# A weight loaded in halves, slot logits spread over two pairs, and zero products in the tail of an attention and mixture-of-experts kernel

## The chip, the cores and the metric

The kernel runs on one core of a Trainium2 chip. A core has TensorE (PE: matrix products, with weight loads shown as PEld), VectorE (DVE), ScalarE (ACT), GpSimd (POOL) and SyncE (SP), which run their own instruction streams and wait for each other by semaphores, and 16 DMA engines that serve all queues. The metric is the device time of one execution in microseconds (us); runs of one kernel are told by their median. The profile is of one execution; its span reaches from the first to the last instruction.

## The reference

Two layers follow each other. The first is causal attention over 4 batches, 8 heads, 768 positions and 64 columns, where some heads see all earlier positions and the others only the first 4 and the last 64. The second is a soft mixture of experts over all 3072 tokens of 512 columns, with 8 experts of 4 slots each:

```python
x = attention(q, k, v).transpose(0, 2, 1, 3).reshape(B * S, H * D)
logits = x @ phi                                   # 3072 x 32
slot_input = softmax(logits, axis=0).T @ x         # 32 slots x 512
for e in range(8):
    h = maximum(slot_input[e] @ w1[e], 0)          # 4 x 1024
    slot_out[e] = h @ w2[e]                        # 4 x 512
out = softmax(logits, axis=1) @ slot_out           # 3072 x 512
```

The slot softmax runs over all tokens, so no expert can start before attention has ended. The inputs are float32: q, k and v have 18.9 MB, w1 and w2 together 33.6 MB. The output has 6.3 MB.

## The kernel before

**Attention** runs over 16 pairs of heads (`n`, four to a batch). A pair's scores are cut into six groups (`g`): `qk` makes the scores of one group and their exponentials on ACT (lines 116 to 135), `mask` zeroes what a head does not see (DVE), and `pvmm` multiplies by v with an appended column of ones (line 159). q, k and v come with rows in partitions and are turned on PE: `transpose` (line 85) into a PSUM tile of the pool `trp`, which has two buffers and serves seven kinds of tile in rotation, and `evac` copies it to SBUF. While pair `n` is computed, q, k and v of pair `n + 1` are turned, in groups 2, 3 and 4; the transposes follow the group's scores and precede its value products. `norm` divides by the column of sums into `xb`, the attention output; `x_transpose` and `evac_x` make its transpose `xT`, one pair behind.

**Slot work inside the loop.** Batch `b` is done when pair `4b + 3` is. In the following pairs, with `bt = (n - 4) % 4`, its logits are made: `slot_logits(b, c)` (lines 188 to 201) multiplies phi by half of `xT` on PE, takes the exponential on ACT and copies it on POOL into `expT`. Both halves run in the pair with `bt == 1`, after groups 0 and 3. `xT` has one buffer. `slots_to_tokens(b)` turns the exponentials (six small transposes) in group 1 of the pair with `bt == 2`, and `dispatch(b)` uses them with `xb` in group 1 of the pair with `bt == 3`. The last batch has a way of its own behind the loop.

**Order.** The order of each engine's instructions is written out by hand. Loads other than the first q and phi are issued from POOL's queue, which casts them to bf16, in program order: k and v of pair 0, the identity (a memset and a select), q, k and v of pair 1, those of pairs 2 and 3 in one transfer each, then one weight at the head of most pairs (`w_order`, line 311) and the loads of two later pairs at the head of odd pairs. The buffers of q, k and v lie in what are w2[5] to w2[7] later, so these three weights are issued last, after the transposes of pair 15. w2[6] and w2[7] come in halves of 256 columns: both left halves, then both right ones. A weight w1 lands with 8,192 B to a partition.

**The tail.** `layer1` makes the hidden rows of all experts from w1, `h_transpose` turns them, and `layer2(e, c0, cl)` adds eight products of expert e into one PSUM tile `sp` (line 575). When the left half of w2[7] has been used, `slot_cols(0)` scales the left half of the slot outputs on ACT (line 599), `row_sums` makes the token sums of a batch by six products with one column (line 271), and `piece` multiplies `expT` by `slot_out` (line 614), scales on ACT and DVE by turns (lines 617 and 619) and issues the output from SP (line 620). The left halves of batches 0 and 1 are written first, then the right halves, then batches 2 and 3 in whole rows. `warm(count, cols)` issues products of a tile of zeros into a tile that nobody reads.

Of the kernel before, what the change touches and what calls it, by code (L numbers as in the profile page):

```python
# [35 lines left out]
class Attn:  # L36
    def __init__(self, nc, tc, ctx, q, k, v, env):
        self.nc, self.tc = nc, tc
        self.src = {"q": q, "k": k, "v": v}
        self.__dict__.update(env)  # L40
        ent = ctx.enter_context
        self.qkT = ent(tc.tile_pool(name="qkT", bufs=2))
        self.vTp = ent(tc.tile_pool(name="vTp", bufs=1))
        self.ptp = ent(tc.tile_pool(name="ptp", bufs=4))
        self.small = ent(tc.tile_pool(name="small", bufs=2))
        self.xp = ent(tc.tile_pool(name="xp", bufs=2))
        self.xTp = ent(tc.tile_pool(name="xTp", bufs=1))
        self.scp = ent(tc.tile_pool(name="scp", bufs=2, space=PSUM))
        self.trp = ent(tc.tile_pool(name="trp", bufs=2, space=PSUM))
        self.pvp = ent(tc.tile_pool(name="pvp", bufs=1, space=PSUM))  # L50
        self.rawt, self.tp, self.T, self.pT, self.pv = {}, {}, {}, {}, {}
        self.xb, self.xT, self.esl, self.elg, self.lg = {}, {}, {}, {}, {}
# [223 lines left out]
def kernel(  # L276
# [23 lines left out]
    w1s = [singles.tile([P, 4, F], BF16, name=f"w1_{e}") for e in range(NE)]  # L300
    w2s = [singles.tile([P, 8, DM], BF16, name=f"w2_{e}") for e in range(NE)]

    def w_load(i, c0=0, cl=DM):
        if i < NE:
            nc.gpsimd.dma_start(w1s[i], moe_w1[i].rearrange("(di do) f -> di do f", do=4))
        else:
            nc.gpsimd.dma_start(w2s[i - NE][:, :, c0:c0 + cl],  # L307
                                moe_w2[i - NE].rearrange("(fi fo) d -> fi fo d", fo=8)[:, :, c0:c0 + cl])


    w_order = [(i,) for i in range(2 * NE - 2)] + [
        (i, c, DM // 2) for c in (0, DM // 2) for i in (2 * NE - 2, 2 * NE - 1)]

    ident = singles.tile([P, P], BF16, name="ident")
# [15 lines left out]
    with ExitStack() as actx:  # L330
        asing = actx.enter_context(tc.tile_pool(name="asing", bufs=1))
        slot_acc = asing.tile([P, DM], F32, name="slot_acc")
        slot_bf = asing.tile([P, DM], BF16, name="slot_bf")
# [17 lines left out]
        at = Attn(nc, tc, actx, q, k, v, env)  # L351
# [14 lines left out]
        nc.gpsimd.memset(ident, 1.0)  # L366
        nc.gpsimd.affine_select(ident, ident, pattern=[[-1, P]], compare_op=ALU.is_equal,
                                fill=0.0, base=0, channel_multiplier=1)
        at.load(1)
        at.load(2, pairs=2)  # L370

# [50 lines left out]
        for n in range(NP):  # L422
            if n % 2 and n + 3 < NP:
                at.load(n + 3, pairs=2)
            for _ in range(0 if n % 4 == 3 or n > 13 else len(w_order) - 5 if n == 13 else 1):
                w_load(*w_order.pop(0))
            if n == 1:

                nc.gpsimd.memset(sum4, 1.0)
                for g in range(4):  # L430
                    nc.gpsimd.affine_select(sum4[32 * g:32 * (g + 1)], sum4[32 * g:32 * (g + 1)],
                                            pattern=[[-1, ES]], compare_op=ALU.is_equal,
                                            fill=0.0, base=0, channel_multiplier=1)
                phf = at.small.tile([P, 4, ES], F32, tag="eb", name="phf", bufs=1)
                nc.sync.dma_start(phf, moe_phi.rearrange("(do di) s -> di do s", di=P))
            for g in range(NG):

                if n or g != 1:
                    at.qk(n, g)
                if n == 0 and g == 0:  # L440
                    at.qk(n, 1)
                last = n == NP - 1

                b, bt = (n - 4) // 4, (n - 4) % 4 if n >= 4 else 0
                if g == 0:
                    if n == 0:
                        at.transpose(0, "v")
                        at.evac(0, "v")
                    else:
                        at.pvmm(n - 1, 4)  # L450
                        at.v_blocks(n)
                        at.evac_blocks(n)
                    at.mask(n, 0)
                elif g == 1:
                    if n:
                        at.pvmm(n - 1, 5)
                    else:
                        at.v_blocks(n)
                        at.evac_blocks(n)
                    if bt == 2:  # L460
                        at.slots_to_tokens(b)
                    elif bt == 3:
                        at.dispatch(b, slot_bf if last else None)
                    if n:
                        at.norm(n - 1, 1)
                elif g == 2:
                    if not last:
                        at.transpose(n + 1, "q")
                    at.pvmm(n, 0)
                    at.mask(n, 1)  # L470
                    if not last:
                        at.evac(n + 1, "q")
                elif g == 3:
                    if not last:
                        at.transpose(n + 1, "k")
                    at.pvmm(n, 1)
                    at.mask(n, 2)
                    if not last:
                        at.evac(n + 1, "k")
                elif g == 4:  # L480
                    if not last:
                        at.transpose(n + 1, "v")
                    at.pvmm(n, 2)
                    if not last:
                        at.evac(n + 1, "v")
                elif g == 5:
                    if n:
                        at.x_transpose(n - 1)
                    at.pvmm(n, 3)
                    if n:  # L490
                        at.evac_x(n - 1)
                    at.norm(n, 0)
                if n == NP - 2 and g == NG - 1:
                    for w in w_order:
                        w_load(*w)
                if n == 0 and g < 2:
                    at.warm(2)
                if bt == 1 and g in (0, 3):
                    at.slot_logits(b, g // 3)
                if (n, g) in MASK_AT:  # L500
                    head_mask(MASK_AT[n, g])
                if n == 2 and g == 0:
                    nc.vector.tensor_copy(phi4.rearrange("p d (g s) -> p d g s", g=4),
                                          phf.rearrange("p d (g s) -> p d g s", g=1).to_broadcast([P, 4, 4, ES]))
                if n == 3 and 2 <= g:
                    gg = g - 2
                    for e4 in range(2):
                        s0 = SPE * (4 * e4 + gg)
                        nc.vector.reduce_sum(emask[32 * gg:32 * (gg + 1), e4:e4 + 1],
                                             sum4[32 * gg:32 * (gg + 1), s0:s0 + SPE], axis=AX.X)  # L510
        n, b = NP - 1, B - 1
# [59 lines left out]
        def layer2(e, c0=0, cl=DM):  # L571
            e4, g = e // 4, e % 4
            for fo in range(8):
                r = fo % 4
                nc.tensor.matmul(sp[32 * r:32 * (r + 1), c0:c0 + cl], hT[e4][:, fo, 32 * g:32 * (g + 1)],
                                 w2s[e][:, fo, c0:c0 + cl], start=(e == 0 and fo < 4),
                                 stop=(e == NE - 1 and fo >= 4), skip_group_check=True)
# [19 lines left out]
        def slot_cols(c):  # L597

            nc.scalar.activation(slot_out[:, 256 * c:256 * (c + 1)], sp[:, 256 * c:256 * (c + 1)], ACT.Copy, scale=rcol)  # L599
# [20 lines left out]
            nc.sync.dma_start(ov[:, r:r + m, c0:c0 + cl], ot[:, o:o + m, c0:c0 + cl])  # L620

        HALF = DM // 2
        for e in (NE - 2, NE - 1):
            layer2(e, 0, HALF)
        slot_cols(0)
        for b in range(2):
            at.row_sums(b)
        for b, r, m in ((0, 0, 1), (0, 1, 2), (0, 3, 3), (1, 0, 3), (1, 3, 3)):
            piece(b, r, m, 0, HALF)
        for b in range(2, B):  # L630
            at.row_sums(b)
        for e in (NE - 2, NE - 1):
            layer2(e, HALF, HALF)
        slot_cols(1)
        for b, r, m in ((0, 0, 1), (0, 1, 2), (0, 3, 3), (1, 0, 3), (1, 3, 3)):
            piece(b, r, m, HALF, HALF)
        for b in range(2, B):
# [37 lines left out]
```

## Time and profile before

| | |
|---|---|
| Median of six runs | 152.33 us (152.13 to 152.92) |
| The profiled execution | 152.92 us, span 151.2 us |
| PE / ACT / DVE / POOL busy | 131.0 / 114.3 / 115.3 / 42.0 us |
| Queue 0 (POOL's loads) | 26.02 MB written, 94.6% of 16 engines' span |
| Queue 1 (SP's loads and outputs) | 6.76 MB, 12.6% |
| HBM read, written | 52.50 MB, 6.29 MB |
| Score exponentials on ACT (lines 129, 133) | 44.3 + 51.8 us |

The page shows the span in 40 slices of 3.78 us. A busy share above 1 for DMA means that packets overlap. The GB/s of a load are counted on the side that is written, in bf16, so that the float32 read is twice as much. The chain of waits follows the last instruction back to what released it at each step. In a timeline a row has start, duration, engine, line, operation, tiles written and read, and in brackets the idle time of the engine before it with what ended it.

### The profile page before, as it was taken

To read this page: it belongs to the slowest core of one execution; us is meant where nothing else is said; L and a number is where in the kernel's file an instruction comes from. 1 tells how busy PE (TensorE), PEld (TensorE's weight loads), DVE (VectorE), ACT (ScalarE), POOL (GpSimd) and SP (SyncE) were. 2 spreads that over 40 slices of the span, in tenths; PEclk is the share of its full clock that TensorE was granted. 3 is DMA by queue.
4 is the path that set the end of the run, shared out by engine and by line. 5 is a ranking of instruction groups with operands and counts; after the bars stand their busy time and mean duration, and the time that the engine had idled before them with its cause. 6 is when DMAs were issued, how large, how long until landed. Compare 5 with 4: busy or idle time off the path is not lost.

```text
span 151.2 us, 5388 instructions
## 1 busy us (share of the span) xinstructions
PE 131.0 (87%) x2312; PEld 83.0 (55%) x2313; DVE 115.3 (76%) x280; ACT 114.3 (76%) x187; POOL 42.0 (28%) x63
## 2 busy tenths in 40 slices
PE   6999898997999999999999999899788992989500
PEld 2457566664657756665775766577364451654100
DVE  6889999899897998988789898788955430548700
ACT  3379899998989999998998999899961530649600
POOL 7917404202455410335554010456400000000000
PEclk9999999999999999999999999999999999556975
DMA  4999999999999999999999999999999999998994
GB/s 112 137 189 206 234 191 213 223 215 203 205 225 198 209 228 219 194 213 224 195 216 220 219 198 208 222 215 212 221 217 215 197 194 197 146 340 296 395 414 187
DMA packets 20327, 33.12 MB, mean 219 GB/s; under 512 B 1616, under 2 KB 17808, under 8 KB 18512
## 3 DMA queue, kind: packets, MB, share of 16 engines
q0 software_dynamic: 15616, 26.02, 94.6%
q1 hardware_dynamic: 4688, 6.76, 12.6%
q8 instruction: 18, 0.29, 0.7%
q14 instruction: 5, 0.04, 0.1%
HBM read 52.50 MB, written 6.29 MB: 389 GB/s over the span
## 4 chain that ended last, share of the span: by engine, by line
DMA 43%; PE 20%; DVE 19%; issue 7%; ACT 3%; POOL 2%; DVEq 0%; POOLq 0%; ACTq 0%
DMA w<-in_k_dram 25%; DMA w<-in_moe_w_dram 16%; PE op L614 4%; DVE xb L172 3%; PE pv L159 3%; DVE pT L143 3%; DVE pT L146 3%; PE sc L124 3%; DVE vb L113 2%; DMA w<-in_q_dram 2%; PE ls L192 2%; PE tpv L85 2%; DVE w L619 2%; DVE xT L186 1%; ACT pT L133 1%
## 5 line engine op out<-in xcount | busy, mean ns | idle before, releaser
L133 ACT ACTIVATE pT<-sc,fb 128x512 bf16<-128x512 f32 (+1 forms) x96 | 51.8, 618 | 3.5 <-PE sc L124 3.0
L129 ACT ACTIVATE pT<-sc 128x1024 bf16<-128x1024 f32 (+1 forms) x48 | 44.3, 953 | 2.7 <-PE sc L124 2.3
L159 PE MATMUL pv<-vb,pT 128*128 128x65 bf16 x672 | 37.0, 194 | 4.2 <-DVE pT L143 2.7
L124 PE MATMUL sc<-qT,kT 64*128 64x256 bf16 (+3 forms) x320 | 34.8, 280 | 0.1
L159 PEld LDWEIGHTS <-pT 128*128 128x128 bf16 x672 | 26.3, 97 | 15.4 <-issue 6.3
L85 PEld LDWEIGHTS <-w 96*64 96x64 bf16 x768 | 19.3, 110 | 11.6 <-issue 8.5
L146 DVE TENSOR_TENSOR pT<-pT,msk 128x1024 bf16<-128x1024 bf16 (+1 forms) x32 | 19.6, 614 | 0.0
L172 DVE TENSOR_TENSOR xb<-pv,rs 128x384 bf16<-128x384 f32 x32 | 17.8, 557 | 1.1
L201 POOL COPY expT<-esl 128x384 bf16<-128x384 bf16 x6 | 11.5, 1910 | 16.5 <-ACT esl L198 16.5
L124 PEld LDWEIGHTS <-kT 64*128 64x128 bf16 x320 | 10.8, 94 | 8.9 <-issue 3.4
L186 DVE COPY xT<-tpx 128x768 bf16<-128x768 bf16 (+1 forms) x17 | 9.1, 535 | 6.8 <-PE tpx L180 6.8
L76 POOL DMA_DIRECT2D w<-in_q_dram x8 | 5.5, 684 | 31.1 <-PE tpq L85 27.7
L143 DVE TENSOR_TENSOR pT<-pT,msk 128x1024 bf16<-128x1024 bf16 x16 | 11.7, 733 | 0.7 <-ACT pT L129 0.7
L619 DVE TENSOR_SCALAR w<-op,rrow 128x256 f32<-128x256 f32 (+1 forms) x18 | 9.5, 570 | 2.9 <-PE op L614 2.7
L101 DVE COPY vT<-tpv 128x768 bf16<-128x768 bf16 x16 | 8.8, 549 | 3.1 <-PE tpv L85 3.0
L614 PE MATMUL op<-slot_out,expT 128*128 128x256 bf16 (+1 forms) x36 | 9.6, 395 | 0.8 <-ACT slot_out L599 0.6
L617 ACT ACTIVATE w<-op,rrow 128x256 f32<-128x256 f32 (+1 forms) x18 | 9.3, 545 | 1.4 <-PE op L614 1.1
L307 POOL DMA_DIRECT2D w<-in_moe_w_dram x10 | 6.7, 675 | 9.5 <-DMA w<-in_moe_w_dram 4.3
L85 PE MATMUL tpk<-ident,w 96*64 96x96 bf16 x256 | 8.5, 209 | 0.7 <-DMA w<-in_k_dram 0.7
L113 DVE COPY vb<-tpb 128x768 bf16<-128x768 bf16 x16 | 8.9, 558 | 0.1
L85 PE MATMUL tpq<-ident,w 96*64 96x96 bf16 x256 | 8.8, 214 | 0.2 <-DVE w L396 0.2
L85 PE MATMUL tpv<-ident,w 96*64 96x96 bf16 x256 | 8.5, 209 | 0.0
(93 smaller groups left out, 148.6 us busy)
## 6 DMA issues: line engine op xcount, KB each, us to landing
w<-in_moe_w_dram POOLq DMA_DIRECT2D x14, 1024.0 KB, 22.0
out_dram<-w SPq DMA_DIRECT2D x4, 768.0 KB, 5.8
w<-in_q_dram POOLq DMA_DIRECT2D x7, 384.0 KB, 16.0
w<-in_k_dram POOLq DMA_DIRECT2D x7, 384.0 KB, 16.7
w<-in_v_dram POOLq DMA_DIRECT2D x7, 384.0 KB, 17.3
out_dram<-w SPq DMA_DIRECT2D x6, 384.0 KB, 3.9
w<-in_moe_w_dram POOLq DMA_DIRECT2D x4, 512.0 KB, 24.7
out_dram<-w SPq DMA_DIRECT2D x2, 256.0 KB, 3.3
```

What stands on the lines that cost most here:

```text
L85: self.nc.tensor.transpose(tp[64 * i:64 * (i + 1), s * 96:(s + 1) * 96], src[:96, i, s * 64:(s + 1) * 64], self.ident[:96, :96])
L113: self.nc.vector.tensor_copy(self.vbufs[n % 2][:, :, :, :64], tp.rearrange("p (j h d) -> p h j d", j=6, h=2))
L124: nc.tensor.matmul(sc[:, hh, c:c + ni * P], kT[po:po + 64, j * P:(j + 1) * P], qT[po:po + 64, i0 * P:(i0 + ni) * P], start=True, stop=True)
L129: nc.scalar.activation(pT[:, :, :L], sc[:, :, :L], ACT.Exp, scale=self.scale)
L133: nc.scalar.activation(pT[:, hh, :L], sc[:, hh, :L], ACT.Exp, scale=self.scale, bias=fb[:, h + hh:h + hh + 1])
L143: nc.vector.tensor_mul(v, v, m)
L146: nc.vector.tensor_mul(pT[:, :, :L], pT[:, :, :L], self.msk[:, h:h + 2, c:c + L])
L159: self.nc.tensor.matmul(self.pv[n, lo][:, hh, i % 3, :], pT[:, hh, o:o + P], vb[:, hh, j, :65], start=first, stop=True, skip_group_check=True)
L172: nc.vector.tensor_mul(xo, pv[:, :, :, :64], rs.to_broadcast([P, 2, 3, 64]))
L201: self.nc.gpsimd.tensor_copy(o, e.rearrange("c i (s p) -> c i s p", s=8))
L614: nc.tensor.matmul(op[:, :cl], er[:, r + i, :], slot_out[:, c0:c0 + cl], start=True, stop=True)
L619: nc.vector.tensor_scalar_mul(ot[:, o + i, c0:c0 + cl], op[:, :cl], rr)
```

## The change

- `w_load` takes a range of w1's second axis (`d`), so that w1[0] can be loaded in two transfers. The first half is issued from POOL after the identity and ahead of pair 1; the second takes the place that w1[0] had in `w_order`.
- `xT` gets two buffers. `slot_logits(b, 0)` moves from group 0 to group 3 of the pair with `bt == 1`, and `slot_logits(b, 1)` to group 1 of the next pair. `slots_to_tokens` moves from group 1 to the end of group 4 of that pair.
- The transposes of the next pair are written once ahead of the groups' branches and the evictions once behind them; the order of instructions stays as it was.
- In the tail three zero products of 512 columns stand between the left `layer2` of w2[6] and that of w2[7], two between the right ones. `row_sums(2)` stays ahead of the right products; `row_sums(3)` moves behind `slot_cols(1)`.

```diff
-        self.xTp = ent(tc.tile_pool(name="xTp", bufs=1))
+        self.xTp = ent(tc.tile_pool(name="xTp", bufs=2))
...
         if i < NE:
-            nc.gpsimd.dma_start(w1s[i], moe_w1[i].rearrange("(di do) f -> di do f", do=4))
+            d = slice(c0, min(c0 + cl, 4))
+            nc.gpsimd.dma_start(w1s[i][:, d], moe_w1[i].rearrange("(di do) f -> di do f", do=4)[:, d])
...
-    w_order = [(i,) for i in range(2 * NE - 2)] + [
+    w_order = [(0, 0, 2), (0, 2, 2)] + [(i,) for i in range(1, 2 * NE - 2)] + [
         (i, c, DM // 2) for c in (0, DM // 2) for i in (2 * NE - 2, 2 * NE - 1)]
...
+        w_load(*w_order.pop(0))
         at.load(1)
         at.load(2, pairs=2)
...
+                nxt = None if last_pair else {2: "q", 3: "k", 4: "v"}.get(g)
+                if nxt:
+                    at.transpose(n + 1, nxt)
...
-                    if bt == 2:
-                        at.slots_to_tokens(b)
-                    elif bt == 3:
-                        at.dispatch(b, slot_bf if last else None)
+                    if bt == 3:
+                        at.dispatch(b, slot_bf if last_pair else None)
...
+                if nxt:
+                    at.evac(n + 1, nxt)
...
-                if bt == 1 and g in (0, 3):
-                    at.slot_logits(b, g // 3)
+                if bt == 2 and g == 4:
+                    at.slots_to_tokens(b)
+                if (bt, g) in ((1, 3), (2, 1)):
+                    at.slot_logits(b, bt - 1)
...
-        for e in (NE - 2, NE - 1):
-            layer2(e, 0, HALF)
+        layer2(NE - 2, 0, HALF)
+        at.warm(3, 512)
+        layer2(NE - 1, 0, HALF)
         slot_cols(0)
...
-        for b in range(2, B):
-            at.row_sums(b)
-        for e in (NE - 2, NE - 1):
-            layer2(e, HALF, HALF)
+        at.row_sums(2)
+        layer2(NE - 2, HALF, HALF)
+        at.warm(2, 512)
+        layer2(NE - 1, HALF, HALF)
         slot_cols(1)
+        at.row_sums(3)
```

More of the change, by code (lines that the diff above doesn't have):

```diff
@@ L435 @@
                 nc.sync.dma_start(phf, moe_phi.rearrange("(do di) s -> di do s", di=P))
+            last_pair = n == NP - 1
             for g in range(NG):
@@ L441 @@
                     at.qk(n, 1)
-                last = n == NP - 1
+                nxt = None if last_pair else {2: "q", 3: "k", 4: "v"}.get(g)
+                if nxt:
+                    at.transpose(n + 1, nxt)
                 b, bt = (n - 4) // 4, (n - 4) % 4 if n >= 4 else 0
@@ L466 @@
                 elif g == 2:
-                    if not last:
-                        at.transpose(n + 1, "q")
                     at.pvmm(n, 0)
                     at.mask(n, 1)
-                    if not last:
-                        at.evac(n + 1, "q")
                 elif g == 3:
-                    if not last:
-                        at.transpose(n + 1, "k")
                     at.pvmm(n, 1)
                     at.mask(n, 2)
-                    if not last:
-                        at.evac(n + 1, "k")
                 elif g == 4:
-                    if not last:
-                        at.transpose(n + 1, "v")
                     at.pvmm(n, 2)
-                    if not last:
-                        at.evac(n + 1, "v")
                 elif g == 5:
```

## The prediction

> **What bounds the kernel now.** I read the page's slices first, then the chain of waits from 120 us on, then the engines' busy time in stretches, then PE's timeline where the weights run out.
>
> ```profile
> DMA  4999999999999999999999999999999999998994
> GB/s 112 137 189 206 234 191 213 223 215 203 205 225 198 209 228 219 194 213 224 195 216 220 219 198 208 222 215 212 221 217 215 197 194 197 146 340 296 395 414 187
> ```
>
> The DMA engines are busy from the second slice to the end, but at 112 to 189 GB/s in the first three slices and near 210 after. Loads run until 133.8 us, outputs follow (340 to 414 GB/s).
>
> ```profile
> 104.76 23.73 DMA w<-in_moe_w_dram
> 128.54 0.62 PE sp L575 x8
> 129.15 0.65 PE rp L271 x12
> 129.82 2.75 PE op L614 x11
> ...
> 133.12 0.40 PE rp L271 x6
> 133.52 1.00 PE sp L575 x14
> 134.54 0.48 ACT slot_out L599
> ```
>
> The end hangs on the left halves of the last weight (landed at 128.49). The trace's landings, one per DMA engine, put the right half of it at 128.99 on the first engine, 131.45 at the median, 133.82 on the last. Each engine writes 192 output packets of 1,024 B (the half rows), 49 ns each, and 32 of 6,144 B, 240 ns each: 192 x 0.049 + 32 x 0.240 = 17.1 us. The last engine needs 16.05 us after 133.82, and the last landing is 149.87. The others end at 149.45 to 149.69, having starved about 0.5 us before the right products (issued at 135.98).
>
> ```profile
> 4.00:6.00 2.00, 1.80 (x21) 0.98 (x20) 1.74 (x6) 1.09 (x2) 2.00 (x4) 1.00 1.06 151
> 6.00:8.00 2.00, 2.00 (x30) 0.92 (x27) 1.89 (x9) 0.32 (x1) 1.99 (x4) 1.00 1.12 134
> 8.00:10.00 2.00, 1.67 (x31) 0.97 (x28) 1.43 (x5) 1.94 (x2) 0.00 (x0) 1.00 1.24 183
> 10.00:12.00 2.00, 2.00 (x52) 1.44 (x51) 2.00 (x5) 1.30 (x2) 0.64 (x1) 1.00 1.25 202
> ...
> 124.92:128.34 3.42, 0.92 (x20) 0.32 (x13) 0.00 (x0) 0.00 (x0) 0.00 (x0) 1.00 1.45 198
> 128.34:131.75 3.41, 3.20 (x29) 1.92 (x29) 1.62 (x5) 1.92 (x5) 0.00 (x0) 0.50 0.92 129
> ```
>
> The last columns are the granted clock, DMA share and GB/s. The hole in the loads lies at 4 to 10 us. PE was busy 27% of the stretch before 128.34 and then got half clock until 138.58.
>
> ```profile
> 10.27 0.53 PE L85 MATMUL tpq<-ident,w 96*64 96x96 bf16 x16
> 11.40 0.53 PE L85 MATMUL tpk<-ident,w 96*64 96x96 bf16 x16
> 125.89 0.40 PE L575 MATMUL sp<-w,hT 128*32 128x256 bf16 x8 [0.45 <-DMA w<-in_moe_w_dram]
> 128.54 0.62 PE L575 MATMUL sp<-w,hT 128*32 128x256 bf16 x8 [2.25 <-DMA w<-in_moe_w_dram]
> ```
>
> Pair 1 is transposed at 10.27, 11.40 and 12.54; its q, k, v landed at 9.52, 10.60, 11.69. That margin is only 0.7 to 0.9 us. At the end PE idles 0.45 + 2.25 = 2.70 us for weights.
>
> **Step 1, half of w1[0] first.** The bytes stay; one transfer becomes two. Whole weights land 4.9 us apart, so the half costs 2.45 us of stream. On GpSimd's queue it takes an issue of about 0.57 us (row: 0.58) at 3.50, so the six issues behind it move by that; by 8.6 us all the same bytes are issued. SyncE's queue is untouched.
>
> The gain g is what of the hole it fills. From 6.0 to 10.0 us 561 packets of 1,024 B landed in the queue; at 205 GB/s, less 0.45 us for the 512 small phi packets (about 17 ns each over 16 engines), 3.55 us would carry 711. So 150 packets, 0.75 us, is the upper bound. The lower is 0: if the dip at 6.2 to 7.2 is the delay between an issue at 3.50 and its first packet, the weight starts as late as q did. I take 0.45, nearer the upper, because three issues stood ready by 7 us and the rate was still low.
>
> Here a rule speaks against the split. The Trainium skill, DMA: Bandwidth & Descriptors, section "Anatomy of one DMA — SWDGE (gpsimd) path", gives each transfer a fixed cost of about 2.0 us beside its bytes. By it one transfer more adds 2.0 us and the total below becomes a loss of 1.35. The row: the queued half weights at the end land 2.65 us apart, all 0.524 MB at 198 GB/s, the rate of their stretch; no fixed part shows while the queue is full. I take 0 for it. Packets of 4,096 B do not occur; between the 1,024 B (205 GB/s) and the 8,192 B (217) they cost at most 0.3 us over 1.05 MB; I take 0, with 0.3 in the range.
>
> **Step 2, the stall that it makes.** Pair 1's loads come later by 2.45 less about 0.6 of the dip and the lag: q lands near 11.5 (11.2 to 12.1) against 10.27. PE waits 1.3 to 1.8 us, and behind its transposes stand this pair's value products, the next score product (so ACT), the eviction of qT and the head masks (so DVE). k, v, and pair 2's v (0.41 us ahead now) then fit within 0.3. Stall D = 1.6 us. From pair 4 on the loads are no later than now and D gives them room.
>
> **Step 3, slot logits spread.** Per batch ACT waits for PE's slot products: 2.6 us over 6 places. ACT is the floor of a pair (51.8 + 44.3 us over 16 = 6.0). A pair with both products takes 7.4 to 7.6 us, the next 6.12. One in each can return at most the waits, 2.6 us, and at least nothing; near the low end, 0.5, since ACT's two exponentials stay. The GpSimd copy (1.91 us) now stands ahead of the loads of pairs 10 and 14 and of the last five weight issues. They are covered: a load issued at 50.03 first lands at 64.26, and the queue at 102.55 lasts to 113.5. Uncovered it would cost up to 1.9 us. Two xT buffers cost nothing: xT's waits are all for PE. Slots-to-tokens later in the pair moves six 0.17 us transposes, still a pair ahead of dispatch; a bank wait of 0.3 us per batch at most.
>
> **Step 4, zero products.** Three cost 0.74 us (4 take 0.98), two 0.49. They lie in the 2.70 us of idle. The attention end arrives 1.6 - 0.5 = 1.1 us later; 2.70 - 0.74 - 0.45 = 1.51 stays, so PE is still there before the last left half. Its idle falls to about 0.4 us, and I expect the full clock at 128 us.
>
> A rule to weigh: the Trainium skill, TensorE: Matmul & The Clock Gate, section "HAM oscillation — how this bites in real kernels", asks for no idle gap above about 3.4 us. By it the gap of 2.25 us is harmless and the zeros gain nothing. The row shows a drop after 27% busy, with no gap that long. The row decides: the clock falls somewhere between 27% busy and the 67% of 107.86 to 111.27, which kept it. By the rule the tail gains 0; by the row as follows.
>
> Full clock: sp 0.62 to 0.30, twelve row sums then hide behind slot_out: first output 0.43 us sooner (0 to 0.5). On the right, one row sum behind slot_out and 0.4 for products: issue about 0.4 sooner after the landing of 133.82 - g. ACT and DVE pace the products otherwise (0.47 per two).
>
> **The sum.** Ending engines are the last one (133.82 + 16.05, gains g alone) and the rest (g + 0.4). Since these stand 0.2 to 0.4 us apart, I count 0.2 of the tail. Gain 0.45 + 0.2 = 0.65. Span 151.2 becomes 150.55; the profiled execution took 152.92, 1.7 around its span, so 152.27. It stands 0.59 above the median shown, so I forecast **151.7 us**.
>
> **Rivals.** *The hole moves.* The weight's first packet waits as q's did, g = 0, and the last engine hides the tail: 152.2. For it: rates at 4 to 6 us are low too. Against it: the dip spans three transfers. *The whole hole.* g = 0.75 and the last engine lags less, tail 0.4: 151.2. For it: the median run is shorter than the profiled one. *The early stall drops PE's clock.* The stretch 8.87 to 12.28 is 90% busy; an idle 1.6 us leaves 43%, inside the open 27 to 67%. Half clock for one 3.41 us stretch costs up to 1.7 us, for two 3.4, for three (as in the tail) 5.1. It decides from a late attention end of 2.70 - 0.74 + 0.43 + 0.5 = 2.9 us on; below that the idle, the faster tail and the starving take it. One stretch: 1.1 + 1.7 = 2.8, about 152.3; two: 4.5, so 1.6 over, 154.0. I take 153.2.
>
> **How the numbers follow.** Forecast 0.48 (151.2 to 152.1; five parts in six of it faster); whole hole 0.14; hole moves 0.16; clock 0.22. A measurement here tells 0.3%, 0.46 us, from no change: faster is under 151.87, slower over 152.79. Faster: 0.40 + 0.14 = 0.54; same: 0.08 + 0.13 = 0.21; slower: 0.22 + 0.03 = 0.25. Range 150.9 to 153.3: it leaves out about 0.09 of the clock case above and 0.03 below.
>
> **What would show it.** Step 1: over 180 GB/s in 6 to 10 us, and the last load's landings 0.45 us sooner on every engine. Step 2: PE idle before tpq of pair 1, 1 to 2 us, with the clock at 1.00. Step 3: fewer ACT waits for ls. Step 4: the clock at 1.00 past 128.3, the first output issue near 129.9. I am wrong if q of pair 1 lands after 13, if the clock falls early, or if the last engine's loads don't move.

## The result, and the profile after

| | before | after |
|---|---|---|
| Median | 152.16 us of 72 runs (151.60 to 152.95) | 152.81 us of 35 runs (151.69 to 155.14); a 36th, of 152.47 us, is on record beside them |
| Ratio to before | | 1.0023 (95% interval 1.0008 to 1.0038) |
| Profiled execution | 152.92 us, span 151.2 us | 152.59 us, span 150.9 us |
| Last weight landed, mean of 16 engines / last engine | 130.96 / 133.82 us | 131.04 / 133.87 us |
| Pair 1 / pair 15 turned (first tpq) | 10.27 / 101.71 us | 12.02 / 103.03 us |
| First output issued | 130.77 us | 130.57 us |

The change makes the kernel slightly slower. The 36 executions after it fall into two groups: 22 between 151.69 and 153.35 us (median 152.47), and 14 between 153.88 and 155.14 us (median 154.68), whose mean granted TensorE clock is 0.956 or less; the ratio leaves out those above 153.97 us as slow runs, and no execution before the change is above 152.95 us. So the ratio shows little of the upper group, and the median of all runs shows it. The profiled execution belongs to the first group, and its partner before the change was the slowest of its six runs, so that the two profiles alone show 0.33 us of gain where the runs show none.

The page's slices of the changed kernel:

```profile
PEclk9999999999999999999999999999999999999965
DMA  4999999999999999999999999999999999999994
GB/s 109 145 182 207 212 206 208 227 215 199 206 229 197 211 227 213 201 204 229 197 214 221 215 202 206 224 219 215 215 213 217 203 194 196 157 339 304 391 419 191
```

The clock stays full through the tail, where it fell before, but the load rates of the first three slices (109, 145, 182) are still low. The stretches of the opening that the prediction showed, now of the changed kernel (busy us of PE, PEld, DVE, ACT and POOL, then clock, DMA share and GB/s):

```profile
4.00:6.00 2.00, 1.66 (x22) 0.73 (x20) 1.64 (x6) 1.29 (x2) 2.00 (x4) 1.00 1.03 150
6.00:8.00 2.00, 1.84 (x29) 0.91 (x27) 1.83 (x9) 0.12 (x1) 2.00 (x4) 1.00 1.08 147
8.00:10.00 2.00, 1.67 (x32) 0.96 (x26) 1.46 (x5) 1.93 (x2) 0.61 (x2) 1.00 1.08 181
10.00:12.00 2.00, 0.36 (x5) 0.11 (x4) 1.06 (x2) 0.82 (x2) 0.00 (x0) 1.00 1.36 207
```

In this execution the dip lies at the same time with the half weight in it as it did with pair 1 in it: 150, 147, 181 GB/s against 151, 134, 183. What is new is in the last row: PE has 0.36 us of work in 2 us, where it had 2.00. PE's timeline names the wait:

```profile
12.02 0.53 PE L85 MATMUL tpq<-ident,w 96*64 96x96 bf16 x16 [1.66 <-DMA w<-in_q_dram]
13.15 0.53 PE L85 MATMUL tpk<-ident,w 96*64 96x96 bf16 x16
...
125.11 2.13 PE L571 MATMUL sp<-w,hT 128*32 128x512 bf16 x40
127.40 0.59 PE L61 MATMUL waste<-zeros 128*128 128x512 bf16 x2 [0.16 <-issue]
128.66 0.40 PE L571 MATMUL sp<-w,hT 128*32 128x256 bf16 x8 [0.66 <-DMA w<-in_moe_w_dram]
```

Before pair 1 PE stands 1.66 us for q. At the other end it has 0.16 + 0.66 us of idle left instead of 2.70. The chain of waits from 120 us on hangs on the same load as before:

```profile
108.64 25.23 DMA w<-in_moe_w_dram
133.87 0.04 issue
133.91 0.42 PE sp L571 x8
134.34 0.02 issue
134.36 0.48 ACT slot_out L595
```

So the lead of the engines went from the end of the program to its beginning, and the load that ends the chain arrives when it did.

### The profile page after: what moved, and what is told of

It is laid out like the page before. It is cut to its first block, busy times and chain, and to the rows that moved or that the text cites. A ratio compares the mean times of both kernels' runs of the same rounds, so it can differ in the third digit from the quotient of the medians.

```text
span 150.9 us, 5397 instructions
## 1 busy us (share of the span) xinstructions
PE 129.7 (86%) x2315; PEld 82.5 (55%) x2318; DVE 115.6 (77%) x280; ACT 114.1 (76%) x187; POOL 41.9 (28%) x64
## 4 chain that ended last, share of the span: by engine, by line
DVE 36%; DMA 26%; PE 18%; POOL 7%; issue 5%; ACT 1%; POOLq 1%; DVEq 0%; ACTq 0%
DMA w<-in_moe_w_dram 17%; DMA w<-in_v_dram 9%; DVE xb L172 9%; DVE pT L146 6%; DVE pT L143 5%; DVE xT L186 4%; DVE vb L113 4%; PE pv L159 4%; PE sc L124 4%; PE tpx L180 3%; POOL w L76 3%; PE tpv L85 3%; DVE rs L170 2%; DVE w L615 2%; PE ls L192 2%
## 5 line engine op out<-in xcount | busy, mean ns | idle before, releaser
L146 DVE TENSOR_TENSOR pT<-pT,msk 128x1024 bf16<-128x1024 bf16 (+1 forms) x32 | 21.6, 675 | 0.0
L201 POOL COPY expT<-esl 128x384 bf16<-128x384 bf16 x6 | 12.6, 2107 | 28.5 <-ACT esl L198 28.5
L143 DVE TENSOR_TENSOR pT<-pT,msk 128x1024 bf16<-128x1024 bf16 x16 | 10.9, 681 | 0.0
L61 PE MATMUL waste<-zeros 128*128 128x512 bf16 (+1 forms) x25 | 8.3, 432 | 1.5 <-DVE zeros L366 1.3
L101 DVE COPY qT<-tpq 128x768 bf16<-128x768 bf16 x15 | 8.3, 551 | 1.5 <-PE tpq L85 1.5
L613 ACT ACTIVATE w<-op,rrow 128x256 f32<-128x256 f32 (+1 forms) x18 | 8.7, 543 | 1.0 <-PE op L610 0.9
L610 PE MATMUL op<-slot_out,expT 128*128 128x256 bf16 (+1 forms) x36 | 7.9, 307 | 1.1 <-ACT w L613 0.5
```

Source lines behind the costliest of these rows:

```text
L101: self.nc.vector.tensor_copy(o, i)
L143: nc.vector.tensor_mul(v, v, m)
L146: nc.vector.tensor_mul(pT[:, :, :L], pT[:, :, :L], self.msk[:, h:h + 2, c:c + L])
L201: self.nc.gpsimd.tensor_copy(o, e.rearrange("c i (s p) -> c i s p", s=8))
```

## The experiments

The ratio is always to runs of the kernel before on the same chip, with a 95% interval.

### One part of the change at a time

The first question was which part costs and which part gives. `e1_half_only` adds to the kernel before only the half weight ahead of pair 1:

```diff
...
-    w_order = [(i,) for i in range(2 * NE - 2)] + [
+    w_order = [(0, 0, 2), (0, 2, 2)] + [(i,) for i in range(1, 2 * NE - 2)] + [
...
+        w_load(*w_order.pop(0))
         at.load(1)
...
```

> The kernel before with step 1 alone: the first half of w1[0] ahead of pair 1. Theory S (the moved half delays pair 1 and shortens nothing): PE waits 1.5 to 2.0 us for q of pair 1, the last weight lands within 0.3 us of 133.8 us, attention ends 1.7 to 2.1 us later, and the time is 0.0 to 0.8% above before, with part of the executions near 154.5 us at a lower mean clock (0.94 to 0.955). Theory R (the spread slot products or the tail edits take back a gain of the early half): no loss here, 0.2 to 0.4% faster than before, no executions above 153.5 us.

Measured: 152.42 us (151.78 to 154.38, 22 runs), ratio 1.0022 (1.0001 to 1.0043). Five of the 22 are above 153.4 us. In its profile PE waits 1.20 us for q. It repeats the result of the whole change.

`e2_no_half` is the changed kernel without the half weight (the two added lines above taken out of it):

> The changed kernel without step 1: w1[0] in one transfer in its old place, the slot logits spread, the zeros and the moved row sums kept. Theory S: q of pair 1 meets no wait, attention ends 0.2 to 0.5 us earlier than before, no execution above 153.3 us, ratio 0.994 to 1.000. If three zero products alone keep the clock (PE then idles about 2.2 us of a 3.4 us stretch), the first output is issued near 130.4; if they don't, near 130.8 with the clock at half from 128 us on. Theory R: 0.3% or more above before, as in the changed kernel.

Measured: 152.36 us (151.65 to 152.88, 14 runs), ratio 0.9994 (0.9977 to 1.0012), and nothing above 152.9 us. With the run before, this puts both the loss and the upper group on the half weight; the rest of the change makes neither gain nor loss that these runs show. In the profile the clock fell to half from 129.97 to 140.21 us, zero products and all, after a stretch in which PE was 63% busy.

`e7_tail_only` is the kernel before with the tail alone changed:

```diff
-        for e in (NE - 2, NE - 1):
-            layer2(e, 0, HALF)
+        layer2(NE - 2, 0, HALF)
+        at.warm(3, 512)
+        layer2(NE - 1, 0, HALF)
...
-        for b in range(2, B):
-            at.row_sums(b)
-        for e in (NE - 2, NE - 1):
-            layer2(e, HALF, HALF)
+        at.row_sums(2)
+        layer2(NE - 2, HALF, HALF)
+        at.warm(2, 512)
+        layer2(NE - 1, HALF, HALF)
         slot_cols(1)
+        at.row_sums(3)
```

> The kernel before with step 4 alone: the zero products and the moved row sums in the tail. Theory S with the last DMA engine setting the end: ratio 0.997 to 1.001 although the products of the tail start up to 0.4 us sooner where the clock stays. If the forecast's sum was right that the tail is worth 0.2 us or more by itself: 0.995 to 0.998.

Measured: 152.34 us (151.66 to 152.97, 22 runs), ratio 1.0012 (0.9997 to 1.0028). From the landing of the last left half to the first output issue it took 1.96 us, where the kernel before took 2.28; that 0.3 us does not show in the time.

`e12_slots_only` is the kernel before with the slot logits spread and two `xT` buffers, and neither the half weight nor the zero products:

```diff
-        self.xTp = ent(tc.tile_pool(name="xTp", bufs=1))
+        self.xTp = ent(tc.tile_pool(name="xTp", bufs=2))
...
-                if bt == 1 and g in (0, 3):
-                    at.slot_logits(b, g // 3)
+                if bt == 2 and g == 4:
+                    at.slots_to_tokens(b)
+                if (bt, g) in ((1, 3), (2, 1)):
+                    at.slot_logits(b, bt - 1)
...
```

> The kernel before with steps 2 and 3 alone: two xT buffers, slot logits in two pairs, slots-to-tokens later. Theory S: from pair 1 to pair 15 PE gets through 0.2 to 0.5 us sooner, which the loads hide: ratio 0.998 to 1.001. If the spread products were the loss: 1.002 or above.

Measured: 152.08 us (151.77 to 152.61, 14 runs), ratio 0.9995 (0.998 to 1.001). From pair 1's transposes to those of pair 15 the profiles took 91.27 us in `e7_tail_only` (old slot logits) and 91.02 us in `e2_no_half` (new ones), 0.25 us less. But `e12_slots_only` itself took 91.58 us, against 91.44 before the change, so that this run alone returns nothing there. Whether the spread returns anything is not shown by single profiles.

### How much goes ahead of pair 1

If the half filled a hole, the whole weight would fill more of it and a quarter less. `e4_whole_first` puts all of w1[0] ahead:

```diff
-    w_order = [(0, 0, 2), (0, 2, 2)] + [(i,) for i in range(1, 2 * NE - 2)] + [
+    w_order = [(0, 0, 4)] + [(i,) for i in range(1, 2 * NE - 2)] + [
...
-            for _ in range(0 if n % 4 == 3 or n > 13 else len(w_order) - 5 if n == 13 else 1):
+            for _ in range(0 if n == 0 or n % 4 == 3 or n > 13 else len(w_order) - 5 if n == 13 else 1):
```

> The changed kernel with the whole of w1[0] ahead of pair 1 (size doubled). Theory S: PE waits 4.0 to 4.6 us for q of pair 1, the clock falls to half there in nearly all executions and the profile shows it, the last weight still lands near 133.8, attention ends 5 to 8 us later than before, and the time is 156 to 160 us. If only the stream counted (the forecast's first step), the early dip of the load rate would be filled better and the time would be no worse than with the half.

Measured: 157.02 us (156.59 to 157.45, 6 runs), ratio 1.0296 (1.0273 to 1.032). q of pair 1 landed at 14.41; PE waited 3.35 us and turned it at 14.46, 4.2 us later than before the change; the stretch of the wait was 19% busy and the clock was at half from 13.85 to 24.09 us. Pair 15 was turned at 108.10, 6.4 us late, and the first output left at 134.91, well after the weights. Here the rate from 6 to 10 us did rise, to 204 to 209 GB/s, though it was 120 from 4 to 6 us; yet the last weight landed only some 0.2 us sooner (130.72 as the mean of the engines).

`e9_quarter_first` puts a quarter ahead and leaves three quarters for the old place:

```diff
-    w_order = [(0, 0, 2), (0, 2, 2)] + [(i,) for i in range(1, 2 * NE - 2)] + [
+    w_order = [(0, 0, 1), (0, 1, 3)] + [(i,) for i in range(1, 2 * NE - 2)] + [
```

> The changed kernel with a quarter of w1[0] ahead of pair 1, three quarters in the old place (size halved). Theory S: the quarter is 1.2 us of stream against a margin of 0.75 us, so PE waits 0.3 to 0.8 us for q of pair 1; the stretch keeps more than 67% of work, the clock does not fall, no execution above 153.4 us and none under a mean clock of 0.95 for this reason; ratio 0.999 to 1.001. If every weight ahead of pair 1 costs in proportion, half of the loss of the half weight and a few executions near 154 us.

Measured: 153.03 us (152.56 to 154.60, 10 runs), ratio 1.0064 (1.0033 to 1.0094). A miss: half the bytes do not cost half. PE still waited 1.23 us, the stretch was 54% busy, and the clock was at half from 12.32 to 19.15 us in the profile. The expectation took the quarter as 1.2 us of stream, but q of pair 1 landed 4.2 us after v of pair 0 (11.53 and 7.30 us). That is as late as behind the half (3.6 to 4.6 us in eight profiles); without either it was 1.5 to 2.0. Why a quarter delays q as much as a half, and why even its runs at a higher clock stand at about 152.8 us, is open.

The landings of the last weight, as the mean of the 16 engines, answer the question over all profiles. Seven without the half ahead: 130.96, 130.94, 131.08, 130.96, 130.89, 130.89, 130.73 (mean 130.92). Eight with half or quarter: 131.04, 131.06, 130.97, 131.05, 130.84, 130.98, 130.97, 131.10 (mean 131.00). The loads end no sooner. The last engine's landing alone, which the waits use, spreads from 132.65 to 133.87 us among these and is no measure for a few tenths.

The rates of the opening agree. From 6 to 10 us these eight moved 164 to 193 GB/s and the seven 157 to 182, but from 4 to 6 us the eight moved 112 to 150 and the seven 129 to 162. Over 4 to 14 us the two are nearly equal, 176 to 183 and 175 to 181. The first row is the kernel before; the other four are a later profile of the changed kernel, `e16_after_look`:

```profile
4.00:14.00 10.00, 9.40 (x167) 5.70 (x166) 9.05 (x27) 6.65 (x10) 5.98 (x10) 1.00 1.18 176
...
4.00:6.00 2.00, 1.96 (x20) 0.94 (x19) 1.00 (x4) 1.24 (x2) 2.00 (x5) 1.00 0.97 112
6.00:8.00 2.00, 1.79 (x20) 0.66 (x19) 1.47 (x5) 0.16 (x1) 1.75 (x4) 1.00 1.07 166
8.00:10.00 2.00, 1.97 (x29) 0.92 (x27) 1.50 (x7) 0.99 (x2) 0.83 (x2) 1.00 1.09 195
...
4.00:14.00 10.00, 8.76 (x131) 4.60 (x131) 7.49 (x23) 5.00 (x7) 5.28 (x10) 1.00 1.15 177
```

So the weight moves the hole to an earlier place and does not fill it.

### What makes the dip

`e8_k_first` issues k of pair 0 ahead of the two index patterns on GpSimd, so that the queue is filled earlier:

```diff
+        at.load(0, "k")
         nc.gpsimd.iota(ki, pattern=[[0, 1]], base=0, channel_multiplier=1)
...
-        at.load(0, "kv")
+        at.load(0, "v")
```

> The kernel before with the load of pair 0's k issued ahead of the two iotas on GpSimd, 0.6 us sooner: a gain in the stream of loads that delays no load of a pair. If the loads set the time up to their last landing: the first packets of k near 2.9 us, the last weight lands 0.2 to 0.6 us sooner, ratio 0.996 to 0.999. If the early dip of the rate takes it back, as it did with the half weight, or VectorE's later masks cost it: 1.000 or above.

Measured: 152.05 us (151.32 to 152.62, 14 runs), ratio 0.9995 (0.9976 to 1.0014). As the mean of the engines the last weight landed 0.2 us sooner (130.73), with no gain in the time. The masks that need the index patterns came later: pair 1 was turned at 12.75 and pair 15 at 104.03. So PE came late to the tail, and there the clock stayed full until 142.85 us without the zero products of step 4.

`e10_k_first_no_half` does the same in the changed kernel without the half weight:

> The best parts together: the changed kernel without the early half, and k of pair 0 issued 0.6 us sooner. Theory S: the loads end 0.2 to 0.3 us sooner, the engines keep their lead, ratio 0.996 to 0.999. If the last DMA engine hides it, as it hides the tail: 0.999 to 1.001.

Measured: 152.52 us (151.61 to 153.31, 22 runs), ratio 1.0026 (1.0011 to 1.004), a miss: pair 1 at 12.41, the full clock first at 8.94 us, no gain in the loads (130.96).

`e11_phi_late` takes the 512 small packets of phi out of the dip:

```diff
-                phf = at.small.tile([P, 4, ES], F32, tag="eb", name="phf", bufs=1)
-                nc.sync.dma_start(phf, moe_phi.rearrange("(do di) s -> di do s", di=P))
...
+                if n == 0 and g == 3:
+                    phf = at.small.tile([P, 4, ES], F32, tag="eb", name="phf", bufs=1)
+                    nc.scalar.dma_start(phf, moe_phi.rearrange("(do di) s -> di do s", di=P))
```

> The kernel before with phi's load (512 packets of 128 B) issued from ScalarE in group 3 of pair 0, some 8 us later. It asks what makes the early dip of the load rate. If the small packets do: over 195 GB/s at 8 to 10 us instead of 183, v of pair 1 lands 0.4 to 0.6 us sooner, and the same time is lost after 12 us. If they don't: the rates at 4 to 10 us stay within 10 GB/s. In both the last weight lands as before and the ratio is 0.998 to 1.002, since the same bytes are moved.

Measured: 152.33 us (151.76 to 152.89, 14 runs), ratio 1.0012 (0.9997 to 1.0027). The rates were 145, 139 and 175 GB/s from 4 to 10 us: phi is not the cause of the dip. The transfer that lies in the dip shifts it (above), but 4 to 6 us stayed low with each of them. The cause stays open. This profile also has a half clock from 27.17 to 30.58 us, after a stretch that was 59% busy, and pair 15 turned at 104.38; its time is 152.12 us, so a kernel with the old order of weights can lose the clock early too, and its lead at the end then takes that up.

### Whether the loads bound the end at all

`e5_less_before` leaves the load of w1[3] out of the kernel before, and expert 3 uses w1[2] instead:

```diff
-    w_order = [(i,) for i in range(2 * NE - 2)] + [
+    w_order = [(i,) for i in range(2 * NE - 2) if i != 3] + [
...
-                                     w1s[4 * e4 + g][:, do, c * 512:(c + 1) * 512],
+                                     w1s[2 if 4 * e4 + g == 3 else 4 * e4 + g][:, do, c * 512:(c + 1) * 512],
```

> The kernel before with the load of w1[3] left out (expert 3 uses w1[2], so that expert's rows are wrong): 1.05 MB, 4.9 us less in the stream of loads. It measures how much the engines can spare. Theory S (engines stand 2.70 us ahead of the last weights in the kernel before): the time falls by that and no more, 2.3 to 3.5 us. If the loads alone set the time, it falls by 4.5 to 5.0 us; if the engines do, by less than 0.7 us.

Measured: 150.18 us (149.51 to 150.35, 4 runs), ratio 0.986 (0.9822 to 0.9898), 2.1 us faster. The last weight landed 5.7 us sooner (128.12) and the first output left 3.5 us sooner (127.25), with PE never waiting for a weight. So loads do bound the end, but only for the first 2.1 us; then the engines do: no load stands in the chain of waits from 110 us on.

`e6_less_after` leaves out the same load in the changed kernel, by the same two edits:

> The changed kernel with the load of w1[3] left out in the same way. Theory S (the early stall and the zeros have used up what the engines could spare): the time falls by only 0.4 to 1.6 us, 1 to 2.5 us less than in the kernel before, and part of the executions not at all. If the stall is made good by the spread slot products, it falls as in the kernel before.

Measured: 153.98 us (151.50 to 155.18, 20 runs). Eight runs lie at 151.50 to 151.99 us (median 151.90), and twelve at 153.63 to 155.18 us (median 154.38) with a clock of 0.965 or less. The lower group is 0.6 us below that of the changed kernel (152.47), where the kernel before gained 2.1 us: less lead was left to gain. The upper group moves by only 0.3 us (from 154.68) with 2.1 MB less to read. It is bound by the engines, not by the loads. PE's timeline in its profile (154.67 us):

```profile
12.44 0.53 PE L85 MATMUL tpq<-ident,w 96*64 96x96 bf16 x16 [1.47 <-DMA w<-in_q_dram]
...
130.09 0.59 PE L61 MATMUL waste<-zeros 128*128 128x512 bf16 x2 [0.16 <-issue]
130.62 0.40 PE L571 MATMUL sp<-w,hT 128*32 128x256 bf16 x8
```

The last left products have no wait for a weight in brackets: PE comes to them at 130.62, when even the right half of the weight has landed (129.16).

### What divides the executions

The profile of `e6_less_after` had a half clock from 13.02 to 19.84 us, that of `e1_half_only` from 12.73 to 19.56, and that of the changed kernel none. `e3_stall_zeros` fills the wait with zero products:

```diff
                 nxt = None if last_pair else {2: "q", 3: "k", 4: "v"}.get(g)
+                if n == 0 and g == 2:
+                    at.warm(7, 512)
                 if nxt:
```

> The changed kernel with seven more zero products of 512 columns (1.5 us) ahead of the transposes of pair 1's q, where PE waits for that load. Theory S with the clock: q of pair 1 is turned at the same 12.0 us, the executions above 153.5 us are gone (mean clock 0.97 or more in all), and the median falls to about 152.3. If the slow executions have another cause than PE's idle spell, they stay, about 4 in 10, at a mean clock near 0.945.

Measured: 152.64 us (151.87 to 154.88, 14 runs), ratio 1.0025 (1.0000 to 1.0051). No run has a mean clock below 0.97 (0 of 14, against 14 of 36), so the drop is gone. The median is no better, so the drop is not the whole loss. Three runs are above 153.5 us with a mean clock of 0.977 or more. The profile is of one of them: the full clock was first granted at 10.53 us, pair 1 was turned at 14.42, and one output issue took 1.76 us instead of 0.4.

`e13_later_turn` keeps the changed kernel's loads and turns pair 1 one group later, so that there is less to wait for:

```diff
-                nxt = None if last_pair else {2: "q", 3: "k", 4: "v"}.get(g)
+                nxt = None if last_pair else {2: "q", 3: "k", 4: "v"}.get(g if n else g - 1)
```

> The changed kernel, with q, k and v of pair 1 turned in groups 3, 4 and 5 of pair 0, one group later than now; loads as in the changed kernel. The score and value products of groups 2 and 3 fill the wait, so by the landings of the changed kernel (q 11.97, k 13.10, v 14.02) against the later places (about 11.4, 12.5 and 13.5) about 0.6 us of the stall of 1.75 us is left, in one place or spread. Theory (the stall costs its own length and in some executions a half clock for two stretches; the loads end no sooner): no half clock before 100 us, hardly any execution over 153.3 us with a mean clock under 0.96 (the changed kernel had 14 of 36), transposes of pair 15 near 102.2, last weight landing 133.5 to 133.9, time 152.1 to 152.5, ratio 0.998 to 1.001. Rival (the half weight ahead of pair 1 itself brings the slow executions, by transfers that collide later): four of ten over 153.5 us again. Rival (the stall hid a gain in the loads): ratio 0.995 or less.

Measured: 152.50 us (151.99 to 157.18, 14 runs), ratio 1.0012 (0.9991 to 1.0034). The profile has 0.21 us of wait before tpq in place of 1.66, the clock full from 5.47 to 142.0 us, and pair 15 at 102.73. Twelve runs are at 151.99 to 153.24 us, median 152.32: with the stall nearly gone the order of loads still gains nothing. Two runs are at 156.40 and 157.18 us with a clock of 0.93; no profile shows what happened in them, and 2 of 14 against 14 of 36 is too few to say that the upper group has become rarer. That part of the expectation is not borne out.

The last three runs are single executions of the changed kernel itself, for the phase of the clock's stretches.

> The changed kernel once more, for a look at where the clock's stretches of 3.41 us fall. Theory: the phase of the stretches against the stall (10.36 to 12.02 us) decides. Where one stretch holds the stall whole (it begins between about 8.6 and 10.2 us), PE is under 63% busy in it, the clock is at half for the next 6.8 us, pair 15 is turned at 105 us or later and the time is 153.9 to 155.2. Where a stretch ends inside the stall, both parts are over 67% busy, the clock stays, pair 15 is turned near 103 and the time is 151.7 to 153.3. Rival (the phase does not matter): a half clock with the stall divided, or none with it whole.

> As for the look before: the same kernel, the stretches at another phase. The stall whole in one stretch: half clock behind it and 153.9 to 155.2 us. Divided between two: full clock and 151.7 to 153.3 us.

> As for the two looks before: the same kernel, the stretches at another phase. The stall whole in one stretch: half clock behind it and 153.9 to 155.2 us. Divided between two: full clock and 151.7 to 153.3 us.

Measured: 152.22, 154.23 and 152.36 us. The middle one has the stall whole in one stretch. Its busy times by clock stretch:

```profile
5.99:9.40 3.41, 3.34 (x49) 1.52 (x46) 2.29 (x10) 1.37 (x3) 2.58 (x4) 1.00 1.08 181
9.40:12.81 3.41, 1.69 (x36) 1.19 (x36) 2.09 (x5) 1.73 (x2) 0.00 (x0) 1.00 1.32 207
12.81:16.23 3.42, 3.42 (x55) 2.15 (x52) 2.38 (x7) 1.99 (x4) 1.37 (x2) 0.50 1.25 208
16.23:19.64 3.41, 3.41 (x40) 2.12 (x38) 2.15 (x6) 2.40 (x4) 2.70 (x8) 0.50 1.21 212
19.64:23.05 3.41, 3.03 (x68) 1.99 (x68) 3.38 (x11) 2.90 (x4) 0.00 (x0) 1.00 1.13 202
```

PE is busy 1.69 of 3.41 us (50%) from 9.40 on, and the next two stretches run at 0.50. In the first profile of the changed kernel a stretch ends inside the stall:

```profile
7.64:11.05 3.41, 2.39 (x39) 1.37 (x38) 2.87 (x8) 2.59 (x3) 0.97 (x2) 1.00 1.13 186
11.05:14.47 3.42, 2.46 (x62) 1.78 (x64) 1.90 (x7) 1.37 (x4) 1.19 (x2) 1.00 1.29 206
14.47:17.88 3.41, 3.33 (x72) 2.34 (x68) 3.17 (x10) 3.41 (x7) 2.67 (x9) 1.00 1.25 208
```

Both parts are 70% and 72% busy and the clock stays. The two other executions kept the clock in another way. Their full clock began later (6.66 and 7.20 us); PE came later to the load and waited less:

```profile
11.91 0.53 PE L85 MATMUL tpq<-ident,w 96*64 96x96 bf16 x16 [0.61 <-DMA w<-in_q_dram]
```

In this one (`e16_after_look`) the wait of 0.61 us leaves its stretch 81% busy; in the other 0.98 us leaves 68%. In both the wait lies whole in one stretch and the clock stays, which the expectation had named as the sign of its rival. Here the busy share decides, and the length of the wait enters it as well as its place.

Behind the half clock the lead is gone. PE in the tail of `e15_after_look`, where the left half of the last weight had landed at 127.47 us:

```profile
127.35 2.13 PE L571 MATMUL sp<-w,hT 128*32 128x512 bf16 x40
129.41 0.82 PE L61 MATMUL waste<-zeros 128*128 128x512 bf16 x3
130.16 0.40 PE L571 MATMUL sp<-w,hT 128*32 128x256 bf16 x8
```

The products that need it start at 130.16, 2.7 us after the weight, behind 0.8 us of zero products that now fill nothing. Pair 15 was turned at 105.28, against 102.99 and 102.83 in the other two executions, and the spans are 152.5 against 150.5 and 150.6 us.

## Why the prediction was wrong

It gave 151.7 us and faster as the likeliest. The kernel is slower by 0.2 to 0.4% (by the ratio and by the medians of all runs). Three terms failed: the gain g of step 1 (0.45 us taken, 0 measured), the 0.2 us of the tail (0 measured), and the reckoning that the lead at the end covers the stall, which left out what the stall does to the clock (some 2.2 us in 14 of 36 executions).

**Step 1 failed, in its gain g.** It took 0.45 us of the hole as filled; the runs show 0 (131.00 against 130.92 us for the landing of the last weight, within 0.1 us). The rival that the hole moves was right here. The test that step 1 named for itself, over 180 GB/s in 6 to 10 us, failed in the profile after (147 and 181) but was just met in two of its three later profiles (181 over the four microseconds), and the loads ended no sooner there: what came in at 6 to 10 us was missing at 4 to 6. That three transfers stood ready and the rate was still low was taken as a sign of room. It shows only that the rate was not low for want of work. Its bounds held, with 0 as the lower one. The upper one has a slip: 512 packets of 17 ns over 16 engines are 0.54 us, not 0.45, which makes it 0.66 us instead of 0.75. Its two zeros held too: no loss from the split shows, so that the fixed cost of 2.0 us per transfer, which was weighed there, does not appear in this full queue.

**Step 2 was right in size and wrong in what it costs.** The stall was put at 1.6 us (1.3 to 1.8); in the first profile PE waits 1.66 us and pair 1 is turned 1.75 us later (10.27 to 12.02); in the three later ones PE waits 0.61, 0.98 and 1.45 us. But it was treated as covered by the lead of 2.70 us at the end. In the executions that keep the clock that nearly holds: the lead falls to 0.82 us and the time is 152.47, 0.3 above before. In the others the stall itself drops the clock.

**The rival that the early stall drops PE's clock is what makes the upper group.** It is shown by the clock of 14 of 36 executions, by the profiles of `e1_half_only`, `e6_less_after`, `e9_quarter_first` and `e15_after_look`, and by the absence of low clocks with zeros in the stall. Its mechanism and its open range (27 to 67% busy) were right, and two stretches were among its cases. Its price was off: two stretches were put at 3.4 us, and the three executions show pair 15 later by 2.3 to 2.5 us and the span longer by 1.9 to 2.0. It was then reckoned 1.6 us over, 154.0; the upper group stands at 154.68. It was given 22 in 100 as one case; in fact it comes and goes between executions of one program. What the step left out is the phase: the stretches do not start with the program, and the sum was made with the single profile's phase.

The clock does not explain all of the loss. The lower group stands 0.3 us above the runs before, and `e3_stall_zeros` has a ratio of 1.0025 without a drop. A start that comes late and finds less lead at the end would explain both, and the 1.0026 of `e10_k_first_no_half` too, but no run tests that by itself; it stays open.

**Step 3** said 0.5 us back, 0 to 2.6. ACT's waits for ls went from 2.6 us in 6 places to 1.6 in 3. Up to pair 15 one pair of profiles shows 0.25 us and `e12_slots_only` by itself none. It gives nothing in the time (0.9995), where the loads end the chain.

**Step 4** was right in the trace in its main sign and worth nothing in the time. In the changed kernel the clock stays at 1.00 through 144.17 us. But the zeros alone do not do it: in `e7_tail_only` and `e2_no_half` the stretch at 126.5 to 130 us is 57% and 63% busy and the clock falls. PE's lateness was needed too, and in `e8_k_first` it was enough without zeros. The outputs leave 1.95 us after the left half has landed instead of 2.28, 0.33 of the 0.43 foretold. The sum counted 0.2 of that; the runs of `e7_tail_only` (1.0012) show none of it. Why the end does not follow is not settled: the last landing of an output runs from 148.97 to 149.87 us in the profiles of these two, of the kernels before and after, and of `e12_slots_only`, which has the earliest and has no zeros.

**The sum** stood on one execution of 152.92 us, 0.59 above the median shown. Against the medians its terms would read: 0 for g, 0 for the tail, so 152.2 for the executions that keep the clock (the rival of the hole that moves; measured 152.47), and some 2.2 us more for the rest (154.68 less 152.47).

## What to carry to other kernels

Do not expect bytes that are moved ahead in a queue that always has work to shorten it: here the end of the queue moved by 0.2 us at most, while one weight less brought 2.1 us in the time. Before putting a transfer ahead of others, compare its length in the queue (2.45 us) with the margin by which the next ones land before their use (0.7 to 0.9 us): the difference is a stall, and may be the lesser part of it (1.2 us of quarter weight made a stall of 1.23, not of 0.4). Price such a stall for every phase of the clock's stretches and not for the one in the profile, and look at the spread of the runs before the median: here the engines' lead ahead of the last wait absorbed late work, and the change that spent it showed up as a second group of times.

## What the runs showed of the hardware

- A short stall is enough to lose the clock. Waits of 1.20 to 1.47 us, whole in one stretch of 3.41 us, lost it (`e1_half_only`, `e9_quarter_first`, `e15_after_look`, `e6_less_after`), while one of 1.66 us, divided between two stretches, and one of 0.98 us, whole, did not. In all 18 profiles, from the first full clock up to 115 us, it fell after stretches in which PE was 19, 47, 50, 54, 55 or 59% busy and stayed after all that were 65% or more. The Trainium skill, TensorE: Matmul & The Clock Gate, section "What's actually happening", has a free-running window of 3,413 ns, which the phases here bear out, but names an idle window for the fall; none of these stretches was idle, and the measurement decides.
- In the tail the same count does not divide them. The clock fell after 27, 55, 57 and 63%, but also after 76, 81 and 87% (`e1_half_only` at 132.20 us, `e5_less_before` at 127.44, `e11_phi_late` at 129.57), and it stayed after 55, 60 and 64% (`e3_stall_zeros` at 140.24, `e10_k_first_no_half` at 138.64, `e2_no_half` at 140.21). So the share is no rule for the whole program; why the tail differs is open.
- PE's first instruction stands at 1.26 or 1.27 us in all profiles, and the full clock was first granted at 4.23 to 10.53 us. In each it came at the end of the first stretch in which PE was 87% busy or more; stretches of up to 82% did not bring it. So short gaps at the start can cost one or two stretches, by the phase. The kernel before has 2.70 us of lead for that: its 72 runs stay within 1.4 us of each other.
- The 16 DMA engines drift apart: in the changed kernel the last weight landed at 129.28 us on the first of them and at 133.87 on the last. The wait ends with the last one (133.91), so the landing of this transfer moves by up to 1.2 us between the fifteen profiles above (132.65 to 133.87) while the mean of the engines moves by 0.4 (130.73 to 131.10).
